# Attention pooling and a two-layer network on one core: another cut of the batch into chunks and groups, another order of the first loads, weighted sums moved to VectorE

## The chip, the core and the metric

One core of a Trainium2 chip runs the whole program. The metric is the device time of one execution in microseconds (us), the median of several. The engines are TensorE (PE in the profile, with its weight loads as PEld), VectorE (DVE), ScalarE (ACT), GpSimd (POOL) and SyncE (SP), which here only issues DMAs.

## What is computed

The input `x` has 4 batches of 12480 rows of 128 numbers; there are 32 inducing rows. Cut to what matters:

```python
def mab(q, kv):
    s = scale * (q @ kv.transpose(0, 2, 1))
    s = s - s.max(-1, keepdims=True)
    a = np.exp(s)
    a /= a.sum(-1, keepdims=True) + 1e-09
    return a @ kv
h = mab(I, x)            # 32 x 128 for each batch: a sum over all 12480 rows
y = mab(x, h)            # 12480 x 128 for each batch

t = y.reshape(49920, 128) @ w_in          # 128 x 2048
g = where(t >= 1, t, where(t <= -1, 0, (t + 1)**2 / 4))
out = g @ w_out                           # 2048 x 128
```

`h` of a batch needs the whole batch, so nothing of the second half can start on a batch before all its rows were read. `w_in` and `w_out` come as 64-bit floats and are made single precision on the chip.

## The kernel before, in words

**Chunks and groups.** A batch is cut into 25 chunks (`SIZES`, 15 of 512 rows and 10 of 480). Attention works on groups of up to four chunks (`GROUPS`), since 32 inducing rows fill a quarter of the 128 partitions: four chunks lie one below another and one instruction serves all. The seven groups have 4, 4, 4, 3, 4, 4 and 2 chunks. An instruction on a group costs by the width of a chunk, however many chunks there are.

**First half, `summarize`.** Chunks are loaded (`load`, L630), turned so that features lie on partitions (batch 0 by TensorE, L639, and a copy by ScalarE, L644; later batches by a strided load, L657, and VectorE, L660), scored against the inducing rows (`score`: L682 on TensorE, maximum L687 and bias L690 on VectorE, exponential L699 on ScalarE), and summed with these weights (`gather`: L725 turns the weights, L733 and L735 copy them, L741 multiplies, L748 copies the sum to `hs`). When all seven groups are in, a chain `c1` to `c12` merges them: the maximum over groups (L783, L786, L789), a bias for all (L796, L799), a factor for each group (L802), the total (L805, L806, L809), its inverse (L812, L813), a table of factors for each group (L816), seven matmuls that add the groups (L824), and a copy to `hT` (L828). `multiply` (L850) then forms `h @ w_in` once for the batch; its rounded and rest parts (L855, L858) are spread by 16 small DMAs (`spread`, L870) to the four tiles `hw` that the network's first matmuls take.

**Second half.** `attend` computes for each group the weights of its rows over `h`: L896 on TensorE, then L902, L908, L911 on VectorE, L916 on ScalarE, L919, L925, L933 on VectorE, L922, L928, L939 on GpSimd, L936 on ScalarE, and four DMAs for each chunk (L965) to the tile `aT`. The very first chunk has a shorter way of its own, `attend_first` (L987 to L1030). `chunk` then runs, for each of eight slices `k` of the hidden layer, two matmuls (L1083), their relu (L1091, ScalarE, one instruction for both where the two banks lie side by side, else two), the square (L1077, ScalarE), the bounds (L1096, VectorE, likewise one or two), a rounded part on one of three engines (L1116 GpSimd, L1120 ScalarE, L1122 VectorE), a rest (L1127, GpSimd), and the matmuls of the second layer (L1155); two of the eight slices skip the parts and multiply in full precision. L1167 and L1171 turn and store a chunk.

**What sets the order.** Nothing is ordered by data at run time: `Plan.order` plays the program through with a cost for each operation and gives each engine a fixed list. Among the operations that are ready, the one with the smallest due time goes first; due times come from the tables `DUE` (by kind of operation) and `SHIFT` (by number of a single operation). An engine, and the queue of DMAs on SP, then runs its list strictly in order. `SLOTS` says how many buffers a pool has; a load waits for its buffer. `keep_on` (L1184) adds matmuls of no use where the plan leaves TensorE idle, one each 250 ns from `WARM[0]` on.

**The weights.** `load_f32` reads 256 KB of 64-bit floats and makes 32-bit floats of them: L532 on ScalarE, L537, L540, L546, L552 and L557 on VectorE, L565 or L568 on GpSimd. `w_in` uses the buffers of `hw`, `aT` and `s2`, `w_out` those of the chunks (`w`, `hi`, `lo`), which in batch 0 also take the first loads of `x` (`FIRST`); `w_out` waits for chunk 16 (`after=got_all[0, 16]`). `mask` holds one of the six `hw` buffers until L1023.

## Time and profile before

| what | value |
|---|---|
| median of 3 runs | 1711.74 us (1711.71 to 1712.26) |
| profiled execution | span 1712.0 us from its first to its last instruction; its own time is one of those between 1711.71 and 1712.26 us, so that under 0.3 us lie around the span |
| busy | TensorE 99%, VectorE 95%, ScalarE 96%, GpSimd 95% of the span |
| first network matmul (L1083) | at 64.7 us |
| last stretch | from 1690 us on, TensorE busy 16.5 of 22 us |

The profile is read from its stages: a start in which the engines are loosely filled, until 64.7 us; a long stage in which all four are nearly full; an end of some 20 us. A busy share of TensorE counts matmuls that overlap in its pipeline, so that a full row is no proof that it has no room.

### The profile page before, as it was taken

Reading aid. Unit: us, or ns where it says so; the run is one execution under the profiler, and the core shown is the slowest. Engines: PE = TensorE matmul, PEld = TensorE weight load, DVE = VectorE, ACT = ScalarE, POOL = GpSimd, SP = SyncE. Lnnn points to the kernel's source line nnn. Section 1 sums busy time; section 2 is a strip of 40 time slices with the busy share of each in tenths; the row PEclk is TensorE's granted clock in tenths of the full one; section 3 lists DMA queues with packets and bytes.
Section 4 is the critical chain, followed back from the end, with each engine's and each line's share of the span. In section 5 each row is a group of like instructions: output and inputs, shape, how many; then the busy total and the mean of one; then the engine's idle time right before and its main releaser. Section 6 shows DMA issues by size and latency. Waiting matters only on the chain.

```text
span 1712.0 us, 25022 instructions
## 1 busy us (share of the span) xinstructions
PE 1690.1 (99%) x7716; PEld 1192.6 (70%) x7716; DVE 1633.7 (95%) x2119; ACT 1638.5 (96%) x2380; POOL 1621.4 (95%) x856
## 2 busy tenths in 40 slices
PE   7999999999999999999999999999999999999998
PEld 5756766677766667677776676667777766667776
DVE  5799999999899999999999999999999999999997
ACT  6699999999999999999999999999999999999997
POOL 2599999999999999999999999999999999999998
PEclk9899999999999999999999999999999999999999
DMA  9334433332343233333243333322212111111111
GB/s 275 87 54 81 79 61 65 54 75 50 66 79 74 48 72 66 59 59 70 50 96 54 74 66 69 60 56 55 41 31 58 30 33 36 28 36 36 33 32 18
DMA packets 427095, 105.66 MB, mean 62 GB/s; under 512 B 369842, under 2 KB 412434, under 8 KB 426962
## 3 DMA queue, kind: packets, MB, share of 16 engines
q1 hardware_dynamic: 425874, 103.82, 30.0%
q8 instruction: 61, 1.00, 0.3%
q14 instruction: 72, 0.59, 0.1%
q10 hardware_dynamic: 1088, 0.25, 0.1%
HBM read 48.94 MB, written 25.56 MB: 44 GB/s over the span
## 4 chain that ended last, share of the span: by engine, by line
PE 87%; DVE 6%; ACT 4%; issue 1%; DMA 1%; POOL 0%; SPq 0%; DVEq 0%; ACTq 0%; POOLq 0%
PE banks L1155 61%; PE banks L1083 19%; DVE w L1096 3%; ACT w L1091 2%; ACT w L1077 2%; DVE hi L1122 1%; PE banks L741 1%; PE banks L682 1%; PE banks L896 1%; PE banks L1184 1%; PE banks L725 1%; DMA w<-in_moe_w_out 1%; PE banks L639 1%; DVE oT L1167 1%; PE banks L824 0%
## 5 line engine op out<-in xcount | busy, mean ns | idle before, releaser
L1127 POOL TENSOR_TENSOR lo<-w,hi 128x1024 fp32r<-128x1024 f32 (+1 forms) x599 | 1394.1, 2360 | 20.4 <-PE banks L1155 5.2
L1096 DVE SCALAR_TENSOR_TENSOR w<-banks,w 128x512 f32<-128x512 f32 (+3 forms) x1159 | 953.2, 861 | 22.9 <-ACT w L1077 19.6
L1091 ACT ACTIVATE w<-banks 128x512 f32<-128x512 f32 (+3 forms) x1312 | 832.4, 704 | 22.7 <-PE banks L1083 20.1
L1077 ACT ACTIVATE w<-w 128x1024 f32<-128x1024 f32 (+1 forms) x800 | 826.9, 1068 | 3.1
L1083 PE MATMUL banks<-aT,hw 128*128 128x512 f32 (+1 forms) x1600 | 574.4, 429 | 3.0 <-DVE w L1096 2.1
L1155 PE MATMUL banks<-hi,w_lo 128*128 128x512 f32 (+1 forms) x1198 | 489.5, 409 | 2.9 <-DVE oT L1167 1.5
L1122 DVE TENSOR_REDUCE hi<-w 128x1024 fp32r<-128x1024 f32 (+1 forms) x406 | 474.0, 1176 | 10.8 <-PE banks L1155 1.5
L1155 PE MATMUL banks<-hi,w_hi 128*128 128x512 f32 (+1 forms) x1198 | 464.8, 388 | 0.0
L1155 PE MATMUL banks<-lo,w_hi 128*128 128x512 f32 (+1 forms) x1198 | 410.5, 428 | 0.1
L1083 PEld LDWEIGHTS banks<-aT,hw 128*128 128x128 f32 x1600 | 294.4, 188 | 151.5 <-DVE w L1096 58.8
L1155 PE MATMUL banks<-w,w_f 128*128 128x512 f32 (+1 forms) x804 | 392.1, 582 | 0.0
L1155 PEld LDWEIGHTS banks<-lo,w_hi 128*128 128x128 f32 x1198 | 222.8, 188 | 104.4 <-issue 52.5
L1155 PEld LDWEIGHTS banks<-hi,w_lo 128*128 128x128 f32 x1198 | 225.3, 188 | 83.6 <-issue 17.7
L1155 PEld LDWEIGHTS banks<-hi,w_hi 128*128 128x128 f32 x1198 | 225.5, 188 | 48.9 <-issue 9.9
L1155 PEld LDWEIGHTS banks<-w,w_f 128*128 128x128 f32 x804 | 151.0, 189 | 61.2 <-issue 37.8
L1116 POOL TENSOR_SCALAR hi<-w 128x1024 fp32r<-128x1024 f32 (+1 forms) x145 | 150.1, 1039 | 5.4 <-ACT s L916 0.8
L1167 DVE STREAM_TRANSPOSE oT<-banks 128x512 f32<-128x512 f32 (+1 forms) x100 | 69.3, 693 | 6.7 <-PE banks L1155 6.0
L660 DVE STREAM_TRANSPOSE xT<-xr 128x512 f32<-128x512 f32 (+1 forms) x75 | 50.7, 678 | 2.2 <-DMA xr<-in_x 2.2
L1120 ACT CAST hi<-w 128x1024 fp32r<-128x1024 f32 (+1 forms) x48 | 50.1, 1045 | 1.2 <-DVE w L1096 1.2
L939 POOL TENSOR_TENSOR a<-a,ahi 128x512 fp32r<-128x512 f32 (+3 forms) x28 | 35.7, 1276 | 2.1 <-ACT ahi L936 2.0
L568 POOL TENSOR_TENSOR w_in_sb<-aT,s 128x256 f32<-128x256 f32 x8 | 6.0, 752 | 31.9 <-DVE aT L557 31.9
L682 PE MATMUL banks<-xT,indT 128*32 128x512 f32 (+1 forms) x200 | 30.5, 612 | 0.0
(113 smaller groups left out, 574.6 us busy)
## 6 DMA issues: line engine op xcount, KB each, us to landing
out<-oT SPq DMA_DIRECT2D x240, 64.0 KB, 2.2
xn<-in_x SPq DMA_DIRECT2D x54, 256.0 KB, 4.1
xr<-in_x SPq DMA_DIRECT2D x180, 64.0 KB, 2.8
out<-oT SPq DMA_DIRECT2D x158, 60.0 KB, 2.2
aT<-ahi SPq DMA_DIRECT2D x118, 64.0 KB, 2.0
aT<-a SPq DMA_DIRECT2D x118, 64.0 KB, 2.0
xn<-in_x SPq DMA_DIRECT2D x30, 240.0 KB, 4.2
xr<-in_x SPq DMA_DIRECT2D x120, 60.0 KB, 2.6
```

The lines of the kernel that those rows point to most:

```text
L660: nc.vector.transpose(make(xT[b, c])[:, : CW[c]], xr.tile[:, : NB[c]].rearrange("c n i -> c (n i)"))
L682: nc.tensor.matmul(p[q * M : (q + 1) * M, :cw], indT, xT[b, c].tile[:, :cw], start=True, stop=True)
L1077: nc.scalar.activation(w.tile[:, :, :cw], w.tile[:, :, :cw], AF.Square, scale=0.5)
L1083: nc.tensor.matmul(make(h)[:, :cw], hw[b][ft // 4].tile[:, ft % 4 * P : (ft % 4 + 1) * P], aT[b, c].tile[:, :cw], start=True, stop=True,)
L1091: each(of, i, hs_, lambda h, to: nc.scalar.activation(to, h, AF.Relu, bias=1.0), cw, w)
L1096: lambda h, t: nc.vector.scalar_tensor_tensor(t, h, 1.0, t, op0=ALU.max, op1=ALU.min), cw, w,
L1116: nc.gpsimd.tensor_scalar(make(hi)[:, :, :cw], w.tile[:, :, :cw], 1.0, 0.0, op0=ALU.mult, op1=ALU.add)
L1120: nc.scalar.copy(make(hi)[:, :, :cw], w.tile[:, :, :cw])
L1122: nc.vector.tensor_reduce(make(hi)[:, :, :cw], w.tile[:, :, :cw].unsqueeze(3), axis=AX.X, op=ALU.max)
L1127: nc.gpsimd.tensor_sub(make(lo)[:, :, :cw], w.tile[:, :, :cw], hi.tile[:, :, :cw].bitcast(F32))
L1155: nc.tensor.matmul(acc.tile[:, :cw], wt[k][:, i, :], g.tile[:, i, :cw], start=first, stop=(acc.parts == 0),)
L1167: nc.vector.transpose(make(oT)[:, :nb].rearrange("c n i -> c (n i)"), acc.tile[:, :cw])
```

## The change

`SIZES` becomes one chunk of 448, sixteen of 512 and eight of 480 rows, and `GROUPS` the first chunk by itself and six full groups of four. In batch 0 the lone chunk keeps its own first way (now 448 wide), and the group attention starts with the next group. In batches 1 to 3 (`apart`) the lone chunk is laid on the four quadrants: `PARTS` and `QUARTER` cut it in four pieces of 128 columns, so that each instruction on it is 128 wide; its rows come by 14 small DMAs instead of one, its `aT` by 16 instead of 4.

The merging chain forms the sum over groups on VectorE (`gathered`, a product and six multiply-adds of 128 x 128, six of them before the last group is in) and then needs one matmul; the bias goes out by one matmul from a row of 128.

`w_out` is loaded to other buffers (`hw`, `aT`, `s2` for even slices, `xr`, `oT` for odd ones) and waits for no chunk; one step of the weights (`to_single`) may go to GpSimd. Loads of batch 1 may not be issued before 54 us of the plan. The plan takes 4.9 us for a first load where it took 3.2. In batch 0 the exponentials go to three buffers in turn. The 16 DMAs of `spread` may go to ScalarE's queue or SP's in batch 0. `keep_on` starts at 1.5 us. `DUE` is changed in most kinds, and `SHIFT` has 2436 entries where it had 880.

```diff
-SIZES = [512] * 15 + [480] * 10
-GROUPS = [[0, 1, 2, 3], [4, 5, 6, 7], [8, 9, 10, 11], [12, 13, 14], [15, 16, 17, 18], [19, 20, 21, 22], [23, 24]]
+SIZES = [448] + [512] * 16 + [480] * 8
+GROUPS = [[0]] + [[c, c + 1, c + 2, c + 3] for c in range(1, 25, 4)]
...
-WARM = (14000, 200)
+WARM = (1500, 250)
...
+    PARTS = [(0, 4), (4, 8), (8, 12), (12, 14)]
+    def apart(b, g):
+        return b > 0 and len(GROUPS[g]) == 1
...
-        made, f = load_f32(src, when, due, after=got_all[0, 16])
+        made, f, value = load_f32(src, when, due, pools=("xr", "oT", "oT") if k % 2 else ("hw", "aT", "s2"))
...
+        later = (54000 if b == 1 else 0, math.inf)
...
+                    def fetch_part(n, c=c):
+                        q, k = divmod(n, 4)
+                        to = (xn[c].tile or make(xn[c], [P, Q, C], F32))[k * M : (k + 1) * M, q, :]
+                        nc.sync.dma_start(to, x_cols(b, c)[:, n, :])
...
-            p1, e1[g] = Slot("h"), Slot("e1")
+            p1, e1[g] = Slot("h"), Slot("e1" if b else ["e1", "hx", "hy"][g % 3])
...
         def c4():
-            p = make(s_b)
-            for q in range(Q):
-                nc.tensor.matmul(p[q * M : (q + 1) * M, :1], mrow, one, start=True, stop=True)
+            nc.tensor.matmul(make(s_b)[:, :1], mrow, one, start=True, stop=True)
...
         def c10():
-            nc.vector.scalar_tensor_tensor(
-                ff, s_f.tile[:, :NG].unsqueeze(2).to_broadcast([P, NG, M]), rs,
-                fold[:, :1, :].to_broadcast([P, NG, M]), op0=ALU.mult, op1=ALU.mult,
-            )
-        def c11(groups):
-            p = s_h.tile or make(s_h)
+            nc.vector.tensor_scalar(share, fold[:, 0, :], rs, None, op0=ALU.mult)
+        def gathered(groups):
+            a = s_a.tile or make(s_a)
             for g in groups:
-                nc.tensor.matmul(p[:, :M], hs[:, g, :], ff[:, g, :], start=(g == 0), stop=(g == NG - 1))
+                to, by = whole if g == NG - 1 else a[:, :C], fr[:, g : g + 1]
+                if g == 0:
+                    nc.vector.tensor_scalar(to, hs[:, g, :], by, None, op0=ALU.mult)
+                else:
+                    nc.vector.scalar_tensor_tensor(to, hs[:, g, :], by, a[:, :C], op0=ALU.mult, op1=ALU.add)
+        def c11():
+            nc.tensor.matmul(make(s_h)[:, :M], whole, share, start=True, stop=True)
...
-            hw_made[b].append([
-                add("ACT" if b == k == r % 2 == 0 else "SP", 610, 2700, end + 3 + k,
+                ways = {e: (610, 2700, end + 3 + k) for e in (["SP"] if b else ["SP", "ACT"])}
...
+    QUARTER = [min(4 * q, CW[0] // M - 4) for q in range(Q)]
...
+            for q in range(rows // M):
+                c, i = (cs[0], QUARTER[q]) if split else (cs[q], 0)
                 nc.tensor.matmul(
-                    p[q * M : (q + 1) * M, :cw], hT[b], xT[b, c].tile[:, :cw], start=True, stop=True
+                    p[q * M : (q + 1) * M, :cw], hT[b], xT[b, c].tile[:, i * M : i * M + cw], start=True, stop=True
                 )
...
-        for g in range(NG):
+        for g in range(0 if b else 1, NG):
             attend(b, g, begins(b, GROUPS[g][0]))
```

Three places of the lists show what moves.

The first is the queue of loads on SP in the start, its last loads of batch 0. In a name, `in_x` is the input, `in_moe_w_in` and `in_moe_w_out` the weights; 96x640 is a chunk of batch 0 with 480 rows, 128x4x128 one of batch 1. Before:

```order
L630 DMA hi_367<-in_x 96x640
L527 DMA w_379<-in_moe_w_out 128x512
L527 DMA w_389<-in_moe_w_out 128x512
L527 DMA hw_402<-in_moe_w_in 128x512
L630 DMA w_413<-in_x 96x640
L630 DMA w_435<-in_x 96x640
L630 DMA lo_446<-in_x 96x640
L630 DMA w_460<-in_x 96x640
L630 DMA w_474<-in_x 96x640
L630 DMA lo_494<-in_x 96x640
L630 DMA xn_505<-in_x 128x4x128
L630 DMA hi_525<-in_x 96x640
```

And changed:

```order
L656 DMA hw_508<-in_moe_w_in 128x512
L778 DMA w_518<-in_x 96x640
L656 DMA hw_539<-in_moe_w_out 128x512
L656 DMA hw_550<-in_moe_w_in 128x512
L656 DMA hw_559<-in_moe_w_out 128x512
L656 DMA xr_575<-in_moe_w_out 128x512
L778 DMA w_581<-in_x 96x640
L778 DMA lo_595<-in_x 96x640
L656 DMA hw_620<-in_moe_w_out 128x512
L656 DMA xr_630<-in_moe_w_out 128x512
L656 DMA hw_669<-in_moe_w_out 128x512
L656 DMA xr_855<-in_moe_w_out 128x512
```

Eight chunks of batch 0 stood behind loads of `w_out`, and two of these (`hi_525` and one further down) behind a load of batch 1 as well; now three loads of `w_out` stand ahead of the last chunk, which is the 37th load, and none of batch 1.

The second is VectorE while the last groups of batch 0 are merged (L806 is the total, L816 the table of factors, L828 the copy to `hT`; between them lie steps of the weights). Before:

```order
L806 TENSOR_REDUCE tot_85<-fs_84 128x1
L546 SCALAR_TENSOR_TENSOR lo_818<-w_753,lo_818 128x256
L812 TENSOR_SCALAR rs_86<-banks 128x1
L813 RECIPROCAL rs_86<-rs_86 128x1
L816 SCALAR_TENSOR_TENSOR ff<-banks,rs_86,fold 128x224
L552 TENSOR_SCALAR hi_806<-lo_818 128x256
L557 SCALAR_TENSOR_TENSOR hi_806<-w_753,hi_806 128x256
L546 SCALAR_TENSOR_TENSOR s_162_798<-hw_730,s_162_798 128x256
L552 TENSOR_SCALAR aT_782<-s_162_798 128x256
L540 TENSOR_SCALAR lo_857<-hi_796 128x256
L828 COPY hT_860<-banks 128x32
```

And changed (L988 is the total, L1005 and L1007 are the weighted sums, L1014 is the copy; L681 to L692 are the steps that were L546 to L557):

```order
L988 TENSOR_REDUCE tot_85<-fs_84 128x1
L681 SCALAR_TENSOR_TENSOR oT_723<-xr_630,oT_723 128x256
L681 SCALAR_TENSOR_TENSOR s_146_757<-hw_559,s_146_757 128x256
L994 TENSOR_SCALAR rs_86<-banks 128x1
L995 RECIPROCAL rs_86<-rs_86 128x1
L998 TENSOR_SCALAR share<-fold,rs_86 128x32
L1005 TENSOR_SCALAR banks<-hs,fr_87 128x128
L1007 SCALAR_TENSOR_TENSOR banks<-hs,fr_87,banks 128x128 x5
L687 TENSOR_SCALAR aT_737<-s_146_757 128x256
L687 TENSOR_SCALAR oT_723<-oT_723 128x256
L692 SCALAR_TENSOR_TENSOR aT_737<-hw_559,aT_737 128x256
L1007 SCALAR_TENSOR_TENSOR whole<-hs,fr_87,banks 128x128
L692 SCALAR_TENSOR_TENSOR oT_723<-xr_630,oT_723 128x256
L1014 COPY hT_857<-banks 128x32
```

Six steps of the weights lie between the total and the copy in both; the seven sums over `hs` have come in among them.

The third is ScalarE between `multiply` and the first relu. Before (L855 rounds the product, L870 spreads it, L1005 is the exponential of the first chunk, L1026 the rounding of its `aT`):

```order
L1005 ACTIVATE s_179_884<-s_179_884 128x128
L855 CAST hx_891<-banks 128x512
L870 DMA hw_899<-hx_891 32x512 x2
L606 CAST w_hi_90<-hi_796 128x256
L606 CAST w_hi_93<-hi_621 128x256
L1026 CAST aT_932<-banks 128x512
```

And changed (the same are L1042, L1058, L1201 and L1225):

```order
L1042 CAST hx_878<-banks 128x512
L1058 DMA hw_887<-hx_878 32x512 x2
L1058 DMA hw_887<-hy_889 32x512 x2
L1058 DMA hw_898<-hy_889 32x512
L1058 DMA hw_898<-hx_878 32x512
L1058 DMA hw_891<-hx_878 32x512
L1201 ACTIVATE s_164_880<-s_164_880 128x128
L666 ACTIVATE oT_941<-xr_855 128x256
L741 CAST w_hi_95<-oT_729 128x256
L741 CAST w_hi_90<-aT_704 128x256
L1058 DMA hw_925<-hx_878 32x512
L741 CAST w_hi_97<-aT_734 128x256
L1225 CAST aT_976<-banks 128x448
```

Seven DMAs stand ahead of the first chunk's exponential on ScalarE where two stood behind it.

## Rows read from the trace of the kernel before

**Rows 1.** The page's first part: busy time of each engine, its share of the span, and its instructions.

```profile
PE 1690.1 (99%) x7716; PEld 1192.6 (70%) x7716; DVE 1633.7 (95%) x2119; ACT 1638.5 (96%) x2380; POOL 1621.4 (95%) x856
```

**Rows 2.** The windows view of the whole program in stretches: from and to (us), length, then for TensorE's matmuls and weight loads, VectorE, ScalarE and GpSimd the busy us and (x instructions), the granted clock (1.00 is 2.4 GHz, 0.50 is 1.2 GHz), the share of the DMA engines and what they moved.

```profile
20.00:45.00 25.00, 23.96 (x344) 16.44 (x345) 16.26 (x45) 19.24 (x50) 5.21 (x7) 1.00 0.93 267
...
48.00:59.00 11.00, 10.36 (x62) 7.83 (x62) 6.73 (x24) 1.81 (x7) 3.94 (x5) 0.53 0.01 1
59.00:65.00 6.00, 5.94 (x52) 4.82 (x49) 4.14 (x13) 2.23 (x5) 2.05 (x4) 1.00 0.31 82
65.00:100.00 35.00, 32.67 (x164) 22.45 (x163) 31.50 (x47) 32.05 (x47) 29.35 (x20) 1.00 0.48 90
100.00:1690.00 1590.00, 1586.36 (x6961) 1119.52 (x6960) 1550.52 (x1937) 1561.78 (x2238) 1563.29 (x806) 1.00 0.29 56
1690.00:1712.00 22.00, 16.54 (x62) 11.03 (x60) 11.93 (x14) 10.20 (x15) 13.97 (x7) 0.97 0.14 22
```

**Rows 3.** The waits view between 100 and 1690 us: who waited for whom, us in total, times, longest.

```profile
PEld banks L1083 <- DVE w L1096: 54.0, 180, 0.8
...
DVE w L1096 <- ACT w L1077: 18.8, 39, 1.3
...
ACT w L1091 <- PE banks L1083: 15.9, 32, 1.4
```

**Rows 4.** The chain that ended last, from 36 to 66 us, in order of time: start us, us, what.

```profile
37.41 1.02 PE banks L639 x10
...
38.98 0.99 PE banks L682 x8
...
40.05 0.67 DVE mg L687
...
41.02 0.76 ACT e L699 x2
...
42.15 4.73 DMA w<-in_moe_w_out
...
49.19 2.28 PE banks L741 x20
51.47 3.13 PE banks L824 x14
...
57.77 1.34 PE banks L850 x8
...
61.32 0.91 PE banks L1023 x8
...
63.62 1.07 PE banks L896 x8
64.69 1.12 PE banks L1083 x4
```

**Rows 5.** The timeline of SyncE's DMA queue in the first 76 us: start us, us that the issues took, and the loads.

```profile
7.38 6.48 SPq L630 DMA_DIRECT2D xn<-in_x  x9
...
16.92 1.00 SPq L630 DMA_DIRECT2D w<-in_x  x2
23.70 0.31 SPq L630 DMA_DIRECT2D lo<-in_x  x1
...
34.34 5.05 SPq L630 DMA_DIRECT2D xn<-in_x  x7
...
69.34 6.08 SPq L657 DMA_DIRECT2D xr<-in_x  x8
```

**Rows 6.** The windows view of two short stretches of the loads, columns as in group 2.

```profile
12.00:18.00 6.00, 5.91 (x29) 3.68 (x27) 4.00 (x12) 3.09 (x7) 1.48 (x2) 1.00 1.05 385
...
22.00:26.00 4.00, 3.95 (x60) 2.36 (x52) 2.17 (x7) 3.40 (x10) 0.00 (x0) 1.00 0.61 151
```

**Rows 7.** The timeline between 9.6 and 10 us, three pieces of VectorE and GpSimd: start us, us, engine, line, operation.

```profile
9.63 0.29 DVE L537 TENSOR_SCALAR aT<-aT 128x256 f32<-128x256 f32 x1
...
9.80 0.74 POOL L568 TENSOR_TENSOR w_in_sb<-aT,s 128x256 f32<-128x256 f32 x1 [8.51 <-DVE aT L557]
...
9.95 0.73 DVE L540 TENSOR_SCALAR s<-aT 128x256 uint32<-128x256 uint32 x1
```

**Rows 8.** The timeline of ScalarE between 57 and 61 us; ACTq is its issuing of DMAs.

```profile
57.53 0.31 ACT L1005 ACTIVATE s<-s 128x128 f32<-128x128 f32 x1 [4.17 <-DVE s L1002]
...
59.84 1.25 ACTq L870 DMA_DIRECT2D hw<-hx  x2
```

**Rows 9.** The groups of instructions between 100 and 1690 us: line, engine, operation, tiles, shapes, count | busy us, mean ns of one | idle time before them and its releasers.

```profile
L939 POOL TENSOR_TENSOR a<-a,ahi 128x512 fp32r<-128x512 f32 (+3 forms) x27 | 34.4, 1274 | 0.1
L928 POOL TENSOR_TENSOR s<-s,sm 128x512 f32<-128x512 f32 (+3 forms) x27 | 27.8, 1031 | 0.7 <-DVE sm L925 0.3 <-PE banks L1083 0.2
L896 PE MATMUL banks<-xT,hT 128*32 128x512 f32 (+1 forms) x184 | 26.9, 592 | 0.0
L741 PE MATMUL banks<-xn,eN 128*32 128x128 f32 (+1 forms) x600 | 22.6, 276 | 0.0
...
L911 DVE TENSOR_TENSOR s<-banks,mx 128x512 f32<-128x512 f32 (+3 forms) x26 | 17.1, 659 | 0.1
...
L733 DVE COPY eN<-banks 128x512 f32<-128x512 f32 (+2 forms) x12 | 7.9, 655 | 0.1
...
L733 ACT COPY eN<-banks 128x512 f32<-128x512 f32 (+3 forms) x9 | 4.9, 543 | 0.0
```

## What is predicted of the change

> **What bounds the kernel now.** Read first the busy shares: TensorE 99%, the three others 95 to 96% [rows 1]. Then the windows, which split the program in stages [rows 2]. Between 100 and 1690 us the engines are busy for 1586, 1551, 1562 and 1563 of 1590 us; ScalarE has 28 us of idle time, GpSimd 27, VectorE 39. No engine is alone the bound there: TensorE's weight loads wait 54 us for VectorE, VectorE 19 us for ScalarE, ScalarE 16 us for TensorE [rows 3]. A microsecond taken from one engine is worth part of a microsecond. The start is another matter. Until the first network matmul at 64.69 us [rows 4] it is a chain: the last chunk of batch 0 is turned at 37.4 us, scored in 0.99, its maximum found in 0.67, its exponential in 0.76; then the chain runs through a load of `w_out` of 4.73 us whose conversion stands ahead of the bias on VectorE; then L741 and the group sums L824, 2.28 and 3.13 us, at a granted clock of 0.53, which is mostly the 1.2 GHz level [rows 2, 4]. ScalarE and GpSimd were busy for only 1.8 and 3.9 us of those 11. What shortens this chain moves the whole rest forward.
>
> **The loads.** Before, nine loads were issued in 6.48 us, 0.72 us each, as fast as the transfers let them (385 GB/s between 12 and 18 us), but SP then stood still from 17.9 to 23.7 us, and the rate fell to 151 GB/s [rows 5, 6]: the loads of `x` share buffers with `w_out` and wait behind it, and seven loads of batch 1 went out at 34.3. In the new list the last chunk is the 37th load and shares no buffer with `w_out`. As before, 12 are issued by 7.4 us; 25 more at 0.72 end at 25.4; landing takes 4.7 [rows 4], so the last chunk is there at about 30. Bounds: 27 if all 9.3 MB came at 385 GB/s, 36 if SP stands still again for the 5.8 us of before, which could happen since three loads of `w_in` and two of `w_out` ahead of it wait for `hw` buffers that VectorE must free. I take 30: VectorE had such work before too, and was busy for 16.3 of 25 us with it [rows 2].
>
> **The chain to hT.** From 30.2: turning 1.0 for two chunks, copy 0.5, scores 1.0, maximum and bias 0.84 [rows 4]; conversions of `w_out` that stand ahead of the last exponential on ScalarE, taken at 1 (bounds 0 and the 4.73 us of a late load): 34.6. Then exponential 0.76, and for each of the two last groups 0.51 for turning (half of 1.02), 0.7 for the copies (one takes 0.54 [rows 9]), and L741 at full clock, half of 2.28: 2.35 each. The last of the seven sums, copies and one matmul in place of L824: five short steps, 1.2 together. Six of the sums (about 1.5 us, estimated from 0.66 us for four times the width [rows 9]) run on VectorE while the last group is being turned, so they cost nothing here; without that cover they would cost the 1.5. That makes 41.2. Two things are added. Waits at the hand-overs: 1 us, as before there were some. And VectorE against GpSimd: at 9.63 us a step of the weights took VectorE 0.29 us, the next, of the same size and begun while GpSimd worked from 9.80 on, took 0.73 and ended as GpSimd did [rows 7]. Six such conversions lie among the sums, with GpSimd now given more of them: bounds 0 and 6 x 0.44 = 2.6 us; I take 1, since only the two of the form that was held up in the row count fully. hT is there at about 43.2; before, L824 ended at 54.6.
>
> The Trainium skill (SBUF — State Buffer, "SBUF: two separate sides") says that VectorE and GpSimd share a pair of ports as an exclusive lock, held for a whole instruction, and that the loser waits; the row of 0.73 us agrees. By that rule taken strictly, the upper bound of 2.6 would hold and the time be 1.6 us later.
>
> **From hT to the first matmul.** The first chunk's scores 0.4, L850 1.0 (1.34 before, partly at the lower clock), rounding 0.6, then on ScalarE seven DMA issues at 1.25 / 2 = 0.62, 4.4 us, which now stand ahead of the exponential of 0.31 [rows 4, 8]. Behind it wait VectorE's five steps (1.6), L1023 (0.91), and rounding and rest (1.3). About 10.5 us, with hand-overs 11.5; before, 10.1. The six issues that left SP's queue save nothing that decides, since the exponential ends later than the spread. The first matmul starts at 43.2 + 11.5 = 54.7; I take 55 against 64.69, **9.7 us gained**, with bounds 4 and 13.
>
> **The ramp.** Chunk 0 has 448 rows instead of 512, so it covers an eighth less of its some 15 us while the next chunks' `aT` is made. SP issued eight strided loads of batch 1 in 6.08 us ahead of those fetches [rows 5]; the new list has ten of them and six small ones there. **2 us lost** (0 to 4).
>
> **The long stage.** The lone chunk takes the place of a group in batches 1 to 3, at a quarter of its width. TensorE: L896 takes 26.9 / 23 = 1.17 us a group (184 matmuls, 8 a group), the scores the same, L741 22.6 / 21 = 1.08 [rows 9]; three quarters of 1.17 + 1.17 + 1.08 + 0.5 for turning is 2.9, and L824 at full clock, 1.6 us, shrinks by 1.4. That is 4.3 us a batch, 13 in three, and 1.2 for the group that batch 0 no longer has: 14. VectorE: six instructions like L911, 0.66 us each, shrink to some 0.28: 2.3 a batch, 7; batch 0 3.3; seven copies to `eN` moved to ScalarE, 4.6; the sums cost 1.5 a batch, 4.5 [rows 9]: 10 less. GpSimd: L939 and L928, 2.3 us, by three quarters, and once in full: 7.5 less. ScalarE: three instructions like its L733 by three quarters, 1.2 a batch and 1.1 once, 4.7 less; seven copies of 0.54 more, 3.8; and by the lists 1146 single relus instead of 1024, 61 pairs split, at 46 ns (the start of one in the plan's cost line) 3: together 2 more. The mean over the four is -7.5. Since ScalarE gives nothing back, I take **6 us gained**; the ends are TensorE's 14 and ScalarE's loss of 2. The extra small DMAs, 25 a batch at 0.62 us, 16 us of SP's 410, hide behind chunks that were fetched earlier.
>
> **Sum.** 1712.0 - 9.7 + 2 - 6 = 1698.3 as a span; the median of the runs lies 0.3 below it: **1698 us**.
>
> **Rivals.**
> 1. The clock falls again in the merging chain. Before, it was granted 0.53 from 48 to 59 us after TensorE had stood with gaps [rows 2]; in the new chain TensorE works in pieces too, with few idle matmuls between them. Then L741, turning and L850 take twice their time: 4 us, 1702. Against it: idle matmuls from 1.5 us on, and shorter gaps. The Trainium skill (TensorE: Matmul & The Clock Gate, "Part 1: The HAM clock gate") says that the throttled clock is the default and activity releases it; the stretch of 0.53 agrees.
> 2. ScalarE sets the pace of the long stage: its load does not fall, so nothing comes of 6: 1704. For it, 96% busy and the split relus; against it, its waits for TensorE.
> 3. TensorE sets the pace: 14 instead of 6, 1690. For it, most of the chain that ended last; against it, the waits on VectorE.
> 4. The loads do not run through: SP stands still for `hw` buffers, x at 36 us, 1704.
> 5. Slower: relus and copies queue ahead of each other on ScalarE in the long stage, banks come free later, and TensorE stands. It decides where the long stage grows by the 7.7 us gained ahead of it and 3.4 more, 11 us; 2 are ScalarE's added load, so its idle time would have to grow from 28 to 37 us, by 0.1 us for each of 100 chunks. With a little more, 1716.
>
> **Chances.** Forecast 0.46, rivals in turn 0.15, 0.14, 0.12, 0.06, 0.07. The three runs differ by 0.6 us; 0.2%, 3.4 us, is about what can be told from no change. All but the last lie below 1708; giving 0.05 of the spread of these to within 0.2% and a part of the last: faster 0.87, same 0.06, slower 0.07. The range 1688 to 1708 takes in the first five and leaves out the last and the tails.
>
> **What would show it.** First matmul of the network at 52 to 58 us; last load of `x` landed by 31; granted clock 1.00 from 30 to 55; the merging chain free of any wait for `w_out`; in the long stage, groups of scores with a 128 wide one in each batch, and TensorE's matmul lines of attention 14 us shorter; about 28 us of ScalarE idle time or less. A first matmul after 60, or an idle time of ScalarE above 35 us, would make the prediction wrong.

## The result, and the profile after

The changed kernel takes 1722.1 us (median of four runs, 1721.0 to 1723.0), the kernel before 1712.0 beside it. By the ratio on record, 1.0069 with a 95% interval of 1.0053 to 1.0085, it is **slower by 0.69%**; these two medians alone make 0.59%. The forecast was 1698, 1688 to 1708. The profiled execution has a span of 1719.5 us and a time of its own of 1721.7.

The busy shares of the changed kernel, answering [rows 1]:

```profile
PE 1694.3 (99%) x7764; PEld 1193.5 (69%) x7764; DVE 1637.3 (95%) x2112; ACT 1645.8 (96%) x2446; POOL 1618.1 (94%) x862
```

Its windows, columns as in [rows 2]:

```profile
20.00:45.00 25.00, 24.47 (x352) 18.67 (x355) 18.82 (x55) 18.75 (x48) 6.81 (x12) 1.00 0.63 169
45.00:51.00 6.00, 5.58 (x69) 4.16 (x60) 5.48 (x16) 2.12 (x5) 3.09 (x4) 1.00 0.15 46
51.00:61.40 10.40, 9.71 (x85) 7.99 (x84) 9.12 (x23) 2.87 (x9) 5.84 (x8) 1.00 0.52 131
...
100.00:1690.00 1590.00, 1575.89 (x6868) 1104.09 (x6867) 1541.89 (x1914) 1556.24 (x2278) 1544.52 (x795) 1.00 0.29 56
```

The shares hardly differ; the windows do. The granted clock stays at 1.00 through the whole start, where it was 0.53 before. Between 100 and 1690 us every engine has *more* idle time: TensorE 14.1 us (3.6 before), VectorE 48 (39), ScalarE 34 (28), GpSimd 45 (27). What grew is not one engine's work.

Two numbers split the result. The first network matmul starts at 61.4 us, 3.2 earlier than the 64.6 before. From there to the end the kernel before takes 1647.4 us, the changed one 1658.1: **+10.7**. I call this time "the rest". To find where it is lost I took the progress of both kernels (columns of hidden layer whose relu is done) and asked how long the changed kernel takes for what the kernel before does in a given stretch:

| stretch of before, us | what it holds | changed kernel |
|---|---|---|
| 90 to 420 | batch 0 | -2.0 |
| 420 to 460 | **merging chain of batch 1** | **+2.1** |
| 460 to 840 | | +3.4 |
| 840 to 880 | **chain of batch 2** | **+1.3** |
| 880 to 1250 | | +1.6 |
| 1250 to 1295 | **chain of batch 3** | **+3.6** |
| 1295 to 1690 | | +2.2 |

In 125 us of batch ends 7.0 us are lost, in the 1475 us between them 5.2; 1.5 come back before 90 us and after 1690. The table has a grain, since the work on neighbouring chunks overlaps: read on the turning of each chunk's output (L1167 before, L1366 changed) the ends lose 5.9 us and the stretches between them 4.5. The third batch end shows how the ends lose it. Timeline of all engines in the changed kernel: start us, us, engine, line, operation, idle time before it and its releaser.

```profile
1270.44 2.25 POOL L1326 TENSOR_TENSOR lo<-w,hi 128x960 fp32r<-128x960 f32 x1 [0.18 <-ACT hi L1319]
1270.59 0.35 DVE L1005 TENSOR_SCALAR banks<-hs,fr 128x128 f32<-128x128 f32 x1
...
1270.98 1.92 DVE L1007 SCALAR_TENSOR_TENSOR banks<-hs,fr,banks 128x128 f32<-128x128 f32 x5
...
1272.66 0.99 POOL L1315 TENSOR_SCALAR hi<-w 128x960 fp32r<-128x960 f32 x1
1272.81 0.85 DVE L987 TENSOR_TENSOR fs<-fr,sg 128x7 f32<-128x7 f32 x1
...
1273.73 2.25 POOL L1326 TENSOR_TENSOR lo<-w,hi 128x960 fp32r<-128x960 f32 x1
1273.78 0.34 DVE L1007 SCALAR_TENSOR_TENSOR whole<-hs,fr,banks 128x128 f32<-128x128 f32 x1
1274.03 0.68 DVE L1366 STREAM_TRANSPOSE oT<-banks 128x480 f32<-128x480 f32 x1
...
1274.17 0.38 PE L991 MATMUL banks<-tot,fold 128*128 128x1 f32 x2 [1.42 <-DVE whole L1007]
...
1274.98 1.03 DVE L998 TENSOR_SCALAR share<-fold,rs 128x32 f32<-128x32 f32 x1
...
1275.94 1.14 DVE L1295 SCALAR_TENSOR_TENSOR w<-banks,w 128x960 f32<-128x960 f32 x1
```

From 1270.6 to 1275.9 VectorE does the chain and turns one chunk's output (L1366, 0.68 us): 5.35 us without one of the network's bounds (L1295), on which TensorE's weight loads wait most [rows 3]. Two of its steps are far longer than their size. `fs` has 128x7 numbers and takes 0.85 us; it ends (1273.66) when GpSimd's L1315 does (1273.65). `share` has 128x32 and takes 1.03; it ends (1276.01) with GpSimd's L1326 (1275.98). TensorE stands for 1.42 us on L991, which is ahead of the network's next matmuls in its list. Then the clock falls; the windows view of the next four us:

```profile
1276.00:1280.00 4.00, 4.00 (x24) 2.02 (x22) 3.16 (x7) 1.35 (x2) 1.51 (x2) 0.57 0.38 61
```

The granted clock is 0.57 there, mostly the 1.2 GHz level, after TensorE had been busy for 2.3 of the 4 us ahead of it. In the kernel before, VectorE's list at the same place interleaves (timeline of VectorE, kernel before):

```profile
1270.46 0.17 DVE L805 TENSOR_TENSOR fs<-banks,sg 128x7 f32<-128x7 f32 x1 [0.23 <-ACT banks L802]
1270.66 0.16 DVE L806 TENSOR_REDUCE tot<-fs 128x1 f32<-128x7 f32 x1
1270.74 1.87 DVE L1096 SCALAR_TENSOR_TENSOR w<-banks,w 128x480 f32<-128x480 f32 x3
1272.52 0.15 DVE L812 TENSOR_SCALAR rs<-banks 128x1 f32<-128x1 f32 x1
1272.70 0.16 DVE L813 RECIPROCAL rs<-rs 128x1 f32<-128x1 f32 x1
1272.90 0.45 DVE L816 SCALAR_TENSOR_TENSOR ff<-banks,rs,fold 128x224 f32<-128x224 f32 x1
```

`fs` takes 0.17 there, and the longest step 0.45: the factors lie in PSUM (`banks`), where the changed kernel has them in SBUF (`fr`).

### The profile page after: what moved, and what is told of

Read it like the earlier page. It is cut to its first block, busy times and chain, and to the rows that moved or that the text cites. A ratio compares the mean times of both kernels' runs of the same rounds, so it can differ in the third digit from the quotient of the medians.

```text
span 1719.5 us, 25317 instructions
## 1 busy us (share of the span) xinstructions
PE 1694.3 (99%) x7764; PEld 1193.5 (69%) x7764; DVE 1637.3 (95%) x2112; ACT 1645.8 (96%) x2446; POOL 1618.1 (94%) x862
## 4 chain that ended last, share of the span: by engine, by line
PE 75%; DVE 9%; ACT 8%; issue 4%; POOL 2%; SPq 0%; DMA 0%; DVEq 0%; ACTq 0%; POOLq 0%
PE banks L1354 53%; PE banks L1282 16%; DVE w L1295 4%; ACT w L1290 4%; ACT w L1276 3%; DVE hi L1321 2%; POOL lo L1326 2%; PE banks L918 1%; PE banks L1090 1%; PE banks L839 1%; DVE oT L1366 1%; PE banks L890 1%; PE banks L1383 1%; PE banks L788 1%; DVE banks L1007 0%
## 5 line engine op out<-in xcount | busy, mean ns | idle before, releaser
L1326 POOL TENSOR_TENSOR lo<-w,hi 128x1024 fp32r<-128x1024 f32 (+2 forms) x599 | 1392.8, 2357 | 26.3 <-DVE hi L1321 8.4
L1295 DVE SCALAR_TENSOR_TENSOR w<-banks,w 128x512 f32<-128x512 f32 (+5 forms) x1140 | 953.0, 875 | 31.0 <-ACT w L1276 24.7
L1290 ACT ACTIVATE w<-banks 128x512 f32<-128x512 f32 (+5 forms) x1373 | 839.3, 678 | 17.6 <-PE banks L1282 14.2
L1276 ACT ACTIVATE w<-w 128x1024 f32<-128x1024 f32 (+2 forms) x800 | 829.4, 1065 | 3.0
L1282 PE MATMUL banks<-aT,hw 128*128 128x512 f32 (+2 forms) x1600 | 584.1, 437 | 7.0 <-DVE w L1295 6.3
L1354 PE MATMUL banks<-hi,w_lo 128*128 128x512 f32 (+2 forms) x1198 | 496.2, 414 | 3.2 <-POOL hi L1315 1.2
L1321 DVE TENSOR_REDUCE hi<-w 128x1024 fp32r<-128x1024 f32 (+2 forms) x404 | 472.5, 1181 | 9.0 <-issue 0.4
L1354 PE MATMUL banks<-hi,w_hi 128*128 128x512 f32 (+2 forms) x1198 | 466.6, 390 | 0.0
L1354 PE MATMUL banks<-lo,w_hi 128*128 128x512 f32 (+2 forms) x1198 | 408.4, 418 | 4.3 <-DVE oT L1366 2.4
L1354 PE MATMUL banks<-w,w_f 128*128 128x512 f32 (+2 forms) x804 | 390.9, 582 | 0.0
L1315 POOL TENSOR_SCALAR hi<-w 128x1024 fp32r<-128x1024 f32 (+2 forms) x146 | 150.7, 1035 | 15.2 <-PE banks L1354 4.6
L1366 DVE STREAM_TRANSPOSE oT<-banks 128x512 f32<-128x512 f32 (+2 forms) x100 | 69.5, 695 | 8.2 <-PE banks L1354 7.1
```

The costliest lines, as they stand in the source:

```text
L1276: nc.scalar.activation(w.tile[:, :, :cw], w.tile[:, :, :cw], AF.Square, scale=0.5)
L1282: nc.tensor.matmul(make(h)[:, :cw], hw[b][ft // 4].tile[:, ft % 4 * P : (ft % 4 + 1) * P], aT[b, c].tile[:, :cw], start=True, stop=True,)
L1290: each(of, i, hs_, lambda h, to: nc.scalar.activation(to, h, AF.Relu, bias=1.0), cw, w)
L1295: lambda h, t: nc.vector.scalar_tensor_tensor(t, h, 1.0, t, op0=ALU.max, op1=ALU.min), cw, w,
L1315: nc.gpsimd.tensor_scalar(make(hi)[:, :, :cw], w.tile[:, :, :cw], 1.0, 0.0, op0=ALU.mult, op1=ALU.add)
L1321: nc.vector.tensor_reduce(make(hi)[:, :, :cw], w.tile[:, :, :cw].unsqueeze(3), axis=AX.X, op=ALU.max)
```

## The experiments

All ratios are to the kernel before, run beside it. "First" is the first network matmul and "rest" the time from it to the end, both of the profiled execution (profiles of before: the one of the front); "ends" are the three batch ends as in the table above, and "between" the four stretches between them together. A dash: the stretches were not taken there. The kernel before is run anew beside each series, and its median moves from 1709.3 to 1712.0 us, so that medians of different rows are not to be subtracted.

| run | ratio (95%) | median us | first | rest | ends | between |
|---|---|---|---|---|---|---|
| before | 1 | 1712.0 | 64.6 | 1647.4 | 0 | 0 |
| changed | 1.0069 (1.0053, 1.0085) | 1722.1 | 61.4 | 1658.1 | +2.1 +1.3 +3.6 | +5.2 |
| sums_on_pe | 1.0082 (1.0067, 1.0097) | 1724.5 | 64.0 | 1659.9 | +1.6 +1.2 +5.4 | +6.0 |
| no_hold | 1.0067 (1.0054, 1.0079) | 1721.7 | 62.0 | 1657.0 | +2.1 +1.3 +2.1 | +5.7 |
| share_psum | 1.0068 (1.0054, 1.0082) | 1720.7 | 61.5 | 1656.4 | +1.2 +1.5 +2.0 | +5.9 |
| share_split | 1.0068 (1.0055, 1.0080) | 1721.4 | 61.5 | 1657.8 | +0.9 +0.5 +4.7 | +6.0 |
| sums_psum | 1.0060 (1.0048, 1.0073) | 1722.0 | 63.4 | 1656.5 | +1.6 +1.6 +2.3 | +5.3 |
| bare_chain | 1.0040 (1.0027, 1.0052) | 1716.7 | 61.5 | 1652.7 | +0.3 -0.1 +0.8 | +6.1 |
| before_sums | 1.0131 (1.0117, 1.0145) | 1733.2 | 63.5 | 1666.3 | +3.6 +6.8 +6.8 | +1.9 |
| act_dose | 1.0056 (1.0043, 1.0069) | 1719.7 | 62.0 | 1656.2 | +2.1 +1.3 +2.1 | +5.0 |
| dve_dose | 1.0062 (1.0050, 1.0075) | 1720.5 | 61.6 | 1656.9 | +2.1 +1.2 +2.0 | +5.9 |
| pe_dose | 1.0043 (1.0030, 1.0057) | 1717.6 | 61.9 | 1653.5 | - | - |
| en_dve | 1.0084 (1.0069, 1.0099) | 1725.6 | 62.3 | 1660.9 | +1.6 +1.5 +2.1 | +9.9 |
| plain_before | 1.0250 (1.0235, 1.0264) | 1753.1 | 61.8 | 1690.2 | - | - |
| plain_after | 1.0302 (1.0287, 1.0317) | 1761.1 | 59.7 | 1702.4 | - | - |
| ind_first | 1.0079 (1.0063, 1.0094) | 1724.2 | 62.8 | 1659.3 | +2.1 +1.3 +3.6 | +6.5 |
| spread_sp | 1.0088 (1.0074, 1.0102) | 1725.6 | 66.0 | 1658.3 | +2.1 +1.3 +3.5 | +5.7 |
| x_first | 1.0072 (1.0059, 1.0085) | 1722.9 | 63.3 | 1658.2 | +2.1 +1.3 +3.6 | +5.5 |
| before_mend | 1.0001 (0.9992, 1.0011) | 1710.7 | 61.9 | 1646.8 | 0.0 +0.2 0.0 | -0.5 |
| before_idle | 1.0000 (0.9991, 1.0009) | 1710.0 | 63.7 | 1645.9 | 0.0 0.0 0.0 | -0.4 |

Cautions for reading it. The four runs of the changed kernel differ by 1.9 us, so 1 us in one row's "first" says little; what is worth reading is the rest. It too is that of one execution: the four kernels that differ in the start alone (changed, ind_first, spread_sp, x_first) have rests of 1658.1 to 1659.3, so that a few tenths say nothing. And the rest holds a coin: **at the third batch end the clock falls in some profiled executions and not in others**. It fell in the changed kernel, ind_first, spread_sp and x_first, whose third end costs 3.5 to 3.6, and stayed at 1.00 in no_hold, act_dose and dve_dose, where the same chain, with the same idle time of TensorE ahead of it, costs 2.0 to 2.1. The fall is worth 1.5 us. Without it the changed kernel's ends would cost 5.5 and its rest be 1656.6, and it is this that a variant with the clock up has to be compared with.

### The chain on VectorE

**sums_on_pe** puts the weighted sums back on TensorE, with seven factors from `fr` in SBUF:

```diff
-            nc.vector.tensor_scalar(share, fold[:, 0, :], rs, None, op0=ALU.mult)
+            nc.vector.scalar_tensor_tensor(ff, fr..., rs, fold..., op0=ALU.mult, op1=ALU.mult)
...
-                    nc.vector.scalar_tensor_tensor(to, hs[:, g, :], by, a[:, :C], ...)
+                nc.tensor.matmul(p[:, :M], hs[:, g, :], ff[:, g, :], ...)
```

> The weighted sums go back to TensorE (seven small matmuls at the place of the one), with every other instruction kept in its place in each queue. Theory A (VectorE's row of chain steps at the three later batch ends holds up bounds, and with them ScalarE and TensorE): the changed kernel falls behind by 6.5 us more than the kernel before in the chunks around 450, 865 and 1275 us; half or more of it comes back, 3 to 7 us, so 1715 to 1719, although TensorE gets 11 us of matmuls more. Theory B (ScalarE, busy for 8 us more, sets the pace of the long stage): ScalarE's work is the same, no change within 1 us, 1721 to 1723. Theory C (TensorE sets it): slower by 3 to 11 us, 1725 to 1733.

None of the three: the rest grew by 1.8, with the clock down in both. `ff` took 0.45, 0.79, 2.17 and 2.31 us in the four batches, `fs` 2.12 in the last. The undo had replaced one held step by a longer one, since the factors stayed in SBUF.

**no_hold** writes `fs` and `share` as another instruction:

```diff
-            nc.vector.tensor_mul(fs, fr, sg)
+            nc.vector.scalar_tensor_tensor(fs, fr, 1.0, sg, op0=ALU.mult, op1=ALU.mult)
...
+            nc.vector.scalar_tensor_tensor(share, fold[:, 0, :], rs, fold[:, 0, :], op0=ALU.mult, op1=ALU.mult)
```

> Only the form of two small steps of VectorE changes: L987 (0.41 and 0.85 us in the last two batch ends, 0.14 in the first) and L998 (1.24, 2.16 and 1.03 us; 0.24 in batch 0) become scalar_tensor_tensor, the form of L1007, whose times did not vary (0.35 to 0.36 us). If they were held up by GpSimd, whose instruction ends within 0.05 us of theirs, they take 0.15 to 0.3 us now: 4.6 us of VectorE over three batch ends. Theory A: 2 to 4 us of it come back, 1718 to 1720. Theory B: within 1 us, 1721 to 1723. If GpSimd was not the cause, the two steps keep their times and nothing changes.

`share` took 1.25, 2.16 and 1.05 us, as before the edit, `fs` up to 0.85; the 1.1 us by which the rest is shorter are the clock, which did not fall. The kind of instruction isn't what holds these steps; the place of their operands was tried next.

**share_psum** gives `share` an operand in PSUM:

```diff
-            nc.vector.reciprocal(rs, rs)
+            nc.vector.reciprocal(s_t.tile[:, 1:2], rs)
+            nc.vector.tensor_mul(share, s_t.tile[:, 1:2].to_broadcast([P, M]), fold[:, 0, :])
```

> The small step L998 took 1.24, 2.16 and 1.03 us at the three later batch ends and each time ended within 0.05 us of an instruction of GpSimd; as a scalar_tensor_tensor with both operands in SBUF it did the same (1.25, 2.16, 1.05). Here it reads the reciprocal from PSUM and stands right behind L995. Theory P (VectorE is held only where all its operands lie in SBUF): about 0.2 us each, 3.7 us of VectorE gone at places where TensorE and ScalarE wait for VectorE, 2 to 4 us back: ratio to before 1.0045 to 1.006. Theory Q (any small step there is held): its time stays near 1 to 2 us, ratio 1.006 to 1.0075.

The same place in its timeline (VectorE and GpSimd):

```profile
1272.51 0.99 POOL L1316 TENSOR_SCALAR hi<-w 128x960 fp32r<-128x960 f32 x1
1272.67 0.85 DVE L987 TENSOR_TENSOR fs<-fr,sg 128x7 f32<-128x7 f32 x1
...
1273.59 2.25 POOL L1327 TENSOR_TENSOR lo<-w,hi 128x960 fp32r<-128x960 f32 x1
...
1274.85 0.19 DVE L996 TENSOR_TENSOR share<-banks,fold 128x32 f32<-128x32 f32 x1
```

GpSimd's instruction runs from 1273.59 to 1275.84 as it did, and `share` passes beside it in 0.19 us; it took 0.19 in all four batches. `fs`, untouched, is still held. **The hold is shown.** Its price is small: the clock was up here, so the ends' 4.7 are to be held against 5.5, and the removal on this step was worth 0.8 us, little more than the table's grain.

**share_split** adds to that: five of the sums are not issued in a row but one behind each of VectorE's next instructions.

```diff
+            spaced[p] = [lambda g=g: gathered([g]) for g in range(1, NG - 1)]
...
             op.emit()
+            if op in spaced:
+                rest, stop = spaced[op], flush[op]
+            elif rest and op.engine == "DVE":
+                rest.pop(0)()
```

> As share_psum, and in batches 1 to 3 the six sums of one piece (2.3 us of VectorE in a row, 0.39 each) are issued one by one, one behind each of VectorE's next instructions. Theory A (VectorE's row of chain steps holds up the bounds behind it): 1 to 3 us more than share_psum come back, ratio 1.003 to 1.005. Rival (VectorE's total is what counts there, not the row): as share_psum, within 1 us.

At two ends it took what was hoped for, +0.9 and +0.5; at the third `fs` came to stand beside another of GpSimd's instructions, was held for 1.86 us, and the clock fell: +4.7. Less the 1.5 of the clock that is 4.6 at the three ends, no better than share_psum: what spacing gained at two, the hold took at one.

**sums_psum** has the sums on TensorE with factors that are made through PSUM:

```diff
+            nc.vector.tensor_scalar(rate, fr, rs, None, op0=ALU.mult)
+            nc.vector.tensor_mul(ff, rate..., fold...)          # rate in PSUM
```

> The changed kernel with the weighted sums on TensorE again, as in sums_on_pe, but the weights ff made right behind L995 from rates that stand in PSUM, as the kernel before had its exponentials in PSUM; nothing is left out. In sums_on_pe this step took 0.79, 2.17 and 2.31 us at the three later batch ends, held by GpSimd, and the undone part brought nothing back. Theory A: ff takes 0.45 us each time, the three batch ends lose 1 to 3 us in all instead of 7, from the first network matmul to the end 1653 to 1655.5, ratio 1.004 to 1.0055. Rival: fourteen matmul instructions in a row on TensorE cost what VectorE gains, 1657 to 1660, ratio 1.0065 to 1.008.

```profile
1271.98 2.25 POOL L1326 TENSOR_TENSOR lo<-w,hi 128x960 fp32r<-128x960 f32 x1 [0.19 <-ACT hi L1319]
1272.13 2.13 DVE L986 TENSOR_TENSOR fs<-fr,sg 128x7 f32<-128x7 f32 x1
...
1275.27 2.26 POOL L1326 TENSOR_TENSOR lo<-w,hi 128x960 fp32r<-128x960 f32 x1
...
1275.72 0.39 DVE L997 TENSOR_TENSOR ff<-banks,fold 128x224 f32<-128x224 f32 x1
```

In this timeline `ff`, 32 times as large as `fs`, passes GpSimd in 0.39 us, and `fs` waits 2.13 for it. The ends cost 5.5, what they cost in the changed kernel with the clock up, and the rest is the same (1656.5 against 1656.6). With 14 matmuls in a row (1.6 us) on TensorE and a held `fs`, taking the sums off VectorE brings nothing back.

**bare_chain** leaves the chain's work out instead: in batches 1 to 3 only two of the seven sums; in all batches no product for `fs`, and `share` from PSUM.

```diff
-            nc.vector.tensor_mul(fs, fr, sg)
-            nc.vector.tensor_reduce(tot, fs, axis=AX.X, op=ALU.add)
+            nc.vector.tensor_reduce(tot, fr, axis=AX.X, op=ALU.add)
...
-            for g in groups:
+            for g in groups if b == 0 else [0] if 0 in groups else [NG - 1]:
```

> The changed kernel with share_psum's step, and with less of VectorE's chain in the three later batch ends: of the seven sums only the first and the last are made, and tot is summed without its product (so the output is not the reference's). VectorE has 2.0 us less in a row at each of the three batch ends, and no small step there can be held. From the first network matmul to the end the changed kernel took 1658.1 us, share_psum 1656.4, the kernel before 1647.4. Theory A (VectorE's chain steps at the batch ends are what costs there, 7 us of the loss lies in 125 us around them): 1650 to 1653. Theory L (the order of the new list costs it, the steps hardly): 1655 to 1657.

The three ends now cost +0.3, -0.1 and +0.8, and the rest is 1652.7, 3.9 below 1656.6. Read on the turned outputs, the ends lose 4.3 in no_hold, with the clock up, and nothing here. The loss at the batch ends is the merging chain's: its sums, its long `share` and its `fs` together, of which only `share` was also taken alone. The loss between the ends, +6.1, is untouched by it and has another cause.

**before_sums** makes the opposite test: the kernel before, with the sums, `fr` and `share` of the changed one and nothing else; they are issued where the plan had the seven matmuls.

```diff
-            nc.scalar.activation(make(s_f)[:, :NG], mg, AF.Exp, bias=nm, scale=SCALE)
+            nc.scalar.activation(fr, mg, AF.Exp, bias=nm, scale=SCALE)
...
-                nc.tensor.matmul(p[:, :M], hs[:, g, :], ff[:, g, :], start=(g == 0), stop=(g == NG - 1))
+                    nc.vector.scalar_tensor_tensor(to, hs[:, g, :], by, a[:, :C], op0=ALU.mult, op1=ALU.add)
```

> The kernel before with one part of the change alone: the weighted sums on VectorE, with fr, share and the sums' result in SBUF as in the change, at the places in VectorE's queue that the matmuls' issue had; every other instruction in its place. From the first network matmul to the end the kernel before took 1647.4 us. Theory A (this part costs the long stage 5 to 7 us): 1652 to 1655. Theory L: 1647 to 1649.5. In batch 0 the chain may end up to 1 us earlier or later.

It is slower by 1.3%, and 17.2 us of the loss lie at the three ends; the four stretches between together lose 1.9. The timelines of VectorE and of GpSimd at its second end, and the waits there (engine and tile waited for: us in total, times, longest):

```profile
861.29 1.98 DVE L818 TENSOR_SCALAR share<-fold,rs 128x32 f32<-128x32 f32 x1
863.19 0.34 DVE L825 TENSOR_SCALAR banks<-hs,fr 128x128 f32<-128x128 f32 x1
863.57 1.92 DVE L827 SCALAR_TENSOR_TENSOR banks<-hs,fr,banks 128x128 f32<-128x128 f32 x5
865.40 2.28 DVE L1101 SCALAR_TENSOR_TENSOR w<-banks,w 128x480 f32<-128x480 f32 x3
```

```profile
860.99 4.41 POOL L1132 TENSOR_TENSOR lo<-w,hi 128x960 fp32r<-128x960 f32 x2 [0.48 <-ACT w L1096]
```

```profile
PE banks L829 <- DVE whole L827: 5.7, 1, 5.7
```

`share` is held until about when the first of GpSimd's two ends, the sums follow, and TensorE, whose list has the one matmul on `whole` ahead of the network's, stands still for 5.7 us. Behind the stands at the three ends the granted clock fell as well (0.62 from 452 to 456 us, 0.50 from 868 to 872 and from 1292 to 1296), so a part of the 17.2 is the clock's; how large a part was not measured. The same chain costs 17.2 us in lists that know nothing of it, with the clock down at all three ends, and in those of the changed kernel 7.0 with it down at one and 5.5 with it up; the kernel before pays nothing of the kind.

### One engine too many?

Three doses take a little from every instruction of a kind, so that the lists stay the same.

```diff
# act_dose
-  nc.scalar.activation(w.tile[:, :, :cw], w.tile[:, :, :cw], AF.Square, scale=0.5)
+  nc.scalar.activation(w.tile[:, :, : cw - 6], w.tile[:, :, : cw - 6], AF.Square, scale=0.5)
# dve_dose: the bounds, cw - 6 wide
# pe_dose: the matmuls on w_lo, 24 columns fewer
+  n = cw - 24 if wt is w_lo and not first else cw
```

> ScalarE's 800 squares leave the last 6 of each half's columns unsquared (1.00 us for 960 elements, so 12 elements are 0.0105 us each): 8.4 us less of ScalarE, spread evenly, and every instruction in its place. Those columns of the output are not the reference's. Theory B (ScalarE's 8 us more of busy time set the slower pace of the long stage): 6 to 8.4 us come back, 1714 to 1716, a ratio to before of about 1.002 to 1.003. Theory L (the order of the changed kernel lets all four engines wait for one another, none is the bound): 1 to 4 us, ratio 1.0045 to 1.006.

> VectorE's 1140 bounds leave out the last 6 columns of each half (0.64 us for 480: 1600 halves by 0.0063 us are 10 us of VectorE less), all else in place; those columns of the output are not the reference's. Theory A2 (VectorE's waits and busy time at the batch ends set it): 5 to 10 us come back, ratio about 1.001 to 1.004. Theory B (ScalarE sets the pace): within 1.5 us, ratio 1.006 to 1.0075. Theory L: 1 to 4 us, ratio 1.0045 to 1.006.

> The changed kernel with the 1198 matmuls of hi by w_lo (but the first of a chunk) 24 columns shorter, 0.010 us each by the 0.22 us between two of 512: 12 us of TensorE less, all else in place (output not the reference's). Rival 3 of the prediction (TensorE sets the pace): 8 to 12 us back, ratio to before 1.000 to 1.002. Theory L (waits go round all engines): 1 to 4 us back, ratio 1.0045 to 1.006; from the first network matmul to the end 1654 to 1657.

The clock was up at the third end in act_dose and dve_dose, so 1656.6 is their base: 8.4 us less of ScalarE shorten the rest by 0.4, 10 less of VectorE lengthen it by 0.3. In pe_dose the clock fell, to 0.91 over 15 us at the third end; 12 less of TensorE shorten the rest by 4.6 against the 1658.1 with a fallen clock. By the ratios, which take in all runs, act_dose lies 0.0013 below the changed kernel, dve_dose 0.0007 and pe_dose 0.0026: 2.2, 1.2 and 4.4 us, the first two within the intervals. So neither ScalarE nor VectorE sets the pace: a microsecond of ScalarE is worth 0.05 to 0.25, one of VectorE 0 to 0.1, one of TensorE about 0.4. GpSimd had no dose. Added work of ScalarE does not explain the loss: the 7.2 us that it is busy longer on the work that the kernel before does from 90 to 1690 us would, at 0.05 to 0.25 each, be 0.4 to 1.8.

**en_dve** tests the copies to `eN` that the change moved to ScalarE; on top of sums_psum, those of batches 1 to 3 go back to VectorE.

```diff
-  copy = nc.scalar.copy if v.engine == "ACT" else nc.vector.tensor_copy
+  copy = nc.scalar.copy if v.engine == "ACT" and b == 0 else nc.vector.tensor_copy
```

> As sums_psum, and in batches 1 to 3 the copies to eN that the change gave to ScalarE are issued by VectorE at the same places (0.68 us each there, 0.54 on ScalarE). Theory B (ScalarE's added work is the rest of the loss, between the batch ends): 1 to 3 us less than sums_psum. Theory L (the rest is in the order's waits; act_dose returned a quarter of what it took away): within 1 us of sums_psum or up to 2 us more.

The rest is 4.4 us longer than that of sums_psum. In these lists, moving them was right.

**plain_before** and **plain_after** empty `SHIFT` in each kernel; plain_after also has the due times of before for all kinds that both have.

```diff
-SHIFT = { "ACT": { 257: -557144, ... } ... }
+SHIFT = {}
```

> The kernel before, its work and due times as they are, without its table of single shifts of due times (SHIFT empty): its order comes from the due times alone. Theory L (the order, not the work, decides the few tenths of a per cent): slower than before by 10 us or more, 1722 to 1760. Theory S (the order matters little): within 4 us, 1708 to 1716.

> The changed kernel's chunks, groups, sums, loads and start, with the due times of the kernel before for the long stage and no table of single shifts, so that its long stage is ordered by the very rules of the run plain_before. Theory L (what the change does to the work is a gain or nothing, its own list of due times and shifts loses it): faster than plain_before by 4 to 15 us. Theory S (the work as the change cuts it, ScalarE's above all, is what costs in the long stage): slower than plain_before by 3 us or more.

plain_before loses 25 to 28 us in the ramp, which hides the comparison of totals. From the turning of chunk 4's output to the end of the program it takes 1565.6 us, plain_after 1588.7 from the same row on. Under these due times the changed work is 23 us worse, and it falls behind chiefly at batch changes (12 us between chunks 48 and 52). The tuned lists of the changed kernel gain 30 us on plain ones (1588.7 to 1558.6), those of before 20 (to 1545.6), so the tables of the change did not gain less than those of before. That the changed work is harder to order is not shown by this: the due times that both plain runs share were made for the kernel before.

### The start

**ind_first** issues the load of the inducing rows first, **x_first** the last three loads of `x` ahead of the loads of weights between them, **spread_sp** all sixteen DMAs of `spread` on SP.

```diff
# ind_first
+    done.sort(key=lambda op: op is not ind_in)
# x_first
+    late = [op for op in loads if op in x_loads][-3:]
+    ahead = loads[loads.index(late[0]) - 1]      # the three go behind this one
# spread_sp
-                queue = nc.scalar if by[0].engine == "ACT" else nc.sync
+                queue = nc.sync
```

> The load of the inducing points is issued first again instead of fifth; all else stays in place. In the changed kernel indT is there at 7.5 us and ScalarE's first copy begins at 9.04; before, 3.0 and about 5.8. Theory S1 (the late indT delays ScalarE's conversions, these the release of the buffers on which SP stands, and so the whole start): first copy at about 6, last x turned 2 to 3 us earlier than 35.1, first network matmul at 58 to 59.5 instead of 61.4, total 1719 to 1720. Theory S2 (the loads or the chain behind them decide): first copy earlier, but first network matmul at 61 or later, total 1721.5 to 1723.

`indT` was made at 7.08 instead of 7.47 us, the first copy at 8.65 instead of 9.04, where S1 needed about 6; so S1 was hardly put to the test, and nothing came of the 0.4 us.

> In the changed kernel the last three loads of x are issued at 24.0, 26.8 and 27.5 us, behind loads of the weights for which SP waits until VectorE has freed a buffer (23.6, 25.0, 26.0). Here these three are issued ahead of the first such load; all else keeps its place. Theory S5 (this stand of SP is what made the chain late: the last x copied at 36.4, hT at 47.6 to 50 in the five profiles so far): the three are issued by 22, the last x copied at 31 to 34, hT at 43 to 46, and all of the gain is kept to the end: ratio to before 1.0035 to 1.005. Theory S6 (the chain waits for VectorE's conversions or for ScalarE's copies anyway): hT at 47 or later, ratio 1.006 to 1.0075.

The loads of `x` were all issued by 23.9 us and landed by 31.5 (35.0 in the changed kernel), but the last copy to `xT` came at 38.1 (36.4 in the changed kernel). Timeline of ScalarE:

```profile
32.03 0.43 ACT L666 ACTIVATE aT<-hw 128x256 f32<-128x256 f32 x1 [2.38 <-DMA hw<-in_moe_w_in]
32.36 1.00 ACT L793 COPY xT<-banks 128x480 f32<-128x480 f32 x2
```

A conversion of `w_in`, whose load had gone behind, stands ahead of those copies in ScalarE's list: 2.38 us of waiting. An earlier landing with the weights' loads where they were was not tried.

> All sixteen spreads of batch 0 are issued by SP instead of eight by ScalarE; every other instruction keeps its place. ScalarE's exponential of the first attention waits 4.8 us behind these issues in the changed kernel (54.61 instead of 49.8). Theory S3 (this wait is on the path to the first network matmul): exponential at about 50, first network matmul at 57 to 58.5 instead of 61.4, total 1717 to 1719.5. Theory S4 (the conversions on VectorE and GpSimd up to 70 us, or SP's queue with eight issues more ahead of the loads of batch 1, decide behind it): first matmul earlier, but chunk 0 done at 91.5 or later (92.4 by rows in the changed kernel is 90.2 for its first chunk), total 1721 to 1724.

With SP alone the exponential of the first chunk came 2.2 us after `hT` instead of 7.0, but the sixteen issues on SP ended at 63.8 and the load of `w_out` behind them landed at 65.8, so that the first matmul came 16.0 us after `hT` instead of 13.8.

**before_mend** and **before_idle** take the kernel before and only mend its start: the first issues two conversions of `w_out` on ScalarE and steps of them on VectorE behind the chain's steps and adds three idle matmuls, the second adds eleven idle matmuls in the merging chain.

```diff
# before_mend
+    move([437, 427], 391)
+    move([438, 428, 429, 430], 403)
+    move([439], 406)
# before_idle
+    for ahead, more in ((395, 4), (397, 2), (401, 5)):
+        at_ = done.index(by_index[ahead])
+        done[at_:at_] = [by_index[117]] * more
```

> The kernel before, all work as it is: around the merging chain of batch 0 two conversions of w_out on ScalarE and four steps of them on VectorE are issued behind the chain's steps instead of ahead, and three idle matmuls more stand before L809. The conversions waited for a load (4.73 us at 42.15) and the chain behind them; and the clock fell to its lower level at 48 us. Expected: nm at 46 instead of 47.6, hT at 50 to 52 instead of 54.8, first network matmul at 60 to 62 instead of 64.6, and the same gain at the end, 3 to 4.5 us: ratio 0.9975 to 0.9985. Rival: the conversions, now later, hold up the first network chunk: no gain, ratio 0.9995 to 1.001.

> The kernel before with eleven idle matmuls more, in TensorE's gaps from 43.5 to 48.6 us. Of 36 runs of the kernel before, 22 have a mean granted clock of 0.999 or 1.000 and take 1707.9 to 1710.5 us, 14 have 0.996 to 0.998 and take 1710.0 to 1714.8; the profile of before is of the second kind. Theory K (in these 14 the clock fell in the merging chain, and this is all their difference): no run below 0.999, all between 1707.5 and 1710.5, ratio to before about 0.999. Rival (the extra matmuls stand in the chain's way): clock up, time not, ratio 1.000 or more.

Both are equal to the kernel before, though the first matmul of before_mend's profile came at 61.9. What they changed is the clock: over the five series of runs the kernel before had a mean granted clock of 0.999 or 1.000 in 39 of 61 runs (1707.3 to 1711.7 us, median 1708.9) and of 0.996 to 0.998 in 22 (1710.0 to 1714.8, median 1712.2); in before_mend (12 runs, median 1710.7) and before_idle (11 runs, median 1710.0) it was never below 0.999. So the fallen clock between 48 and 59 us [rows 2] is a matter of about a third of the runs, it costs them 3 us, and the profiled one was of that third. The medians of the two edits lie 1.8 and 1.1 us above the 1708.9 of the other two thirds, so that they cost about what the clock gives back. No version tried beats the kernel before.

## Why the prediction was wrong

**The loads: wrong by 5 us.** The last load of `x` was to land at 30 us; in the trace it landed at 35.0. SyncE's queue in the changed kernel (start us, us of the issues, loads):

```profile
11.20 1.00 SPq L778 DMA_DIRECT2D xn<-in_x  x2
15.55 0.33 SPq L778 DMA_DIRECT2D w<-in_x  x1
...
20.10 0.42 SPq L778 DMA_DIRECT2D w<-in_x  x1
23.58 0.35 SPq L656 DMA_DIRECT2D hw<-in_moe_w_in  x1
...
27.52 0.33 SPq L778 DMA_DIRECT2D lo<-in_x  x1
```

It was issued at 27.5, not 25.4: SP stood still from 12.2 to 15.5 for a buffer that TensorE freed, and from 20.5 to 23.6 for VectorE. And it took 7.4 us to land, for which the forecast took the 4.7 of a load of weights. The DMA view (tiles, queue, count, KB each, median us from issue to landing) has it in this line:

```profile
lo<-in_x SPq DMA_DIRECT2D x2, 240.0 KB, 7.0
```

So rival 4, with `x` at 36 us, came true within 1 us, less than half of the delay by its stand of SP and the rest by the landing.

**The chain to hT: 43.2 predicted, 47.6 measured, 54.6 before.** The chain of waits of the changed kernel (start us, us, what):

```profile
35.09 1.02 PE banks L788 x10
...
43.56 0.27 DVE banks L1005
43.85 0.37 DVE banks L1007
...
45.49 0.35 DVE banks L1007
...
52.02 0.61 ACTq L1058
...
54.62 0.31 ACT s L1201
```

The six sums that "cost nothing here", because the last group would be turned beside them, stand behind the whole last group instead, in a row on the path: 2.4 us (L1005 and five L1007). That did not make the chain longer than forecast: from the turning of the last chunks (L788, at 35.09, right after the last landing) to `hT` it took 12.5 us, where 13.0 were predicted from 30.2 on. The sums' time was paid by luck, out of the three allowances of 1 us each. The 4.4 missed are thus the late start of the chain; x_first, where the loads landed at 31.5 and the turning still began only at 37.0, behind ScalarE's wait for `w_in`, shows that an earlier landing alone need not bring the chain forward.

**From hT to the first matmul: 11.5 predicted, 13.8 measured.** The mechanism was right up to the exponential: it (54.62) waits for ScalarE's DMA issues, until 7.0 us after `hT`. Behind it the sum left out two terms. The rest of the first chunk's `aT` (L1229) starts at 58.9, 0.8 us after its rounded part was there, since conversions of weights stand ahead of it on VectorE. Then TensorE's list has the scores of two groups ahead of the first network matmul (timeline of TensorE), 1.85 us, where before it had one group in 1.07 [rows 4]:

```profile
59.57 1.92 PE L1090 MATMUL banks<-xT,hT 128*32 128x512 f32 x16 [0.69 <-DVE aT L1229]
61.42 1.28 PE L1282 MATMUL banks<-aT,hw 128*128 128x448 f32 x5
```

That the six issues that left SP "save nothing that decides" was wrong: spread_sp, which gives SP back all eight of ScalarE's, lost 2.2 us by it.

**The start together: 9.7 predicted, 3.2 between the two profiles, about 1 between the medians.** The runs of the kernel before have 1.8 us around their span, not the under 0.3 that was taken, those of the changed one 2.2. The profiled execution of before, with 1712.0 of span, is then one of some 1713.8, above the four runs beside it, and the reading that "the median lies 0.3 below" the span was wrong. With the rest of 1647.4, the median of 1712.0 has its first matmul at 62.8, and that of the changed kernel (1722.1, rest 1658.1) at about 61.8. The forecast took one execution's granted clock of 0.53 [rows 2] for the kernel's own; it is so in a third of the runs.

**The ramp: a loss of 2 predicted.** There was none; the changed kernel is 4.4 us ahead after the first chunk and 5.7 after chunk 20.

**The long stage: 6 gained predicted, 10.7 lost; this is the step that failed.** (The 10.7 is the rest, ramp and end with it.) The two parts of it failed in different ways.

*The savings were there, and little came of them.* The lines that answer to [rows 9], changed kernel, 100 to 1690 us:

```profile
L1090 PE MATMUL banks<-xT,hT 128*32 128x512 f32 (+2 forms) x192 | 23.4, 560 | 0.0
L918 PE MATMUL banks<-xn,eN 128*32 128x128 f32 (+1 forms) x576 | 19.4, 276 | 0.0
...
L1105 DVE TENSOR_TENSOR s<-banks,mx 128x512 f32<-128x512 f32 (+2 forms) x24 | 14.8, 616 | 0.1
```

The attention is 3.5 and 3.2 us lighter in the first two lines and 2.3 in the third, about as costed. But the same groups over the whole program, before and after, show where TensorE's saved time went:

```profile
L1083 PE MATMUL banks<-aT,hw 128*128 128x512 f32 (+1 forms) x1600 | 574.4, 429 | 3.0 <-DVE w L1096 2.1 <-DVE banks L902 0.5 <-DMA hw<-hy 0.2
...
L824 PE MATMUL banks<-ff,hs 128*128 128x32 f32 x56 | 8.6, 302 | 0.0
```

```profile
L1282 PE MATMUL banks<-aT,hw 128*128 128x512 f32 (+2 forms) x1600 | 584.1, 437 | 7.0 <-DVE w L1295 6.3 <-DVE s L1105 0.2
...
L1010 PE MATMUL banks<-share,whole 128*128 128x32 f32 x8 | 1.4, 254 | 0.4 <-DVE whole L1007 0.4
```

The sums are 7.2 us lighter, and 1600 matmuls on the same number of columns are busy 9.7 us longer and idle 4 us longer ahead; what holds them longer was not taken apart. From the first network matmul on, the times of its instructions added up, TensorE has 1.5 us less where 14 were predicted, VectorE 3 where 10 were, GpSimd 9 (predicted 7.5), ScalarE 5 more (2). Of ScalarE's the relus grew by 6.1, for which 3 were taken. My 6 us were a mean over four engines, as if each gave back a fraction of its saving; the doses put that fraction at about 0.4 for TensorE and near nothing for VectorE and ScalarE.

*The cost was in a term that I sized as busy time.* "The sums cost 1.5 a batch" on VectorE. Even as busy time they take 2.6 (0.35, 1.92 and 0.34 us at the third end). Above all they are links of a chain for which TensorE's list holds a place, and they run in a row, with bounds of the network behind them: the three ends lose 5.5 us with the clock up and 7.0 with it down at one, of which bare_chain returns all but 1.0. Part of that is the hold. I had it from [rows 7] and priced it for conversions in the start only; `fs` and `share`, with all operands moved to SBUF by the very change, I did not price at all. In the last batches' chains it took 0.85 us for 128x7 and up to 2.16 for 128x32 numbers.

**The rivals.** The fifth, slower at 1716 for want of banks, had the sign and nearly the size, not the mechanism: it turned on ScalarE's idle time, and that grew to 34 us, short of its 37; en_dve shows that the copies on ScalarE are a gain. The point "idle above 35" did not trip, the point "first matmul after 60" did, at 61.4, and the last `x` landed at 35.0 instead of by 31. Rival 1 (clock falls in the merging chain of the start) did not happen in this profile; at the third batch end it did. Rival 2 is refuted by act_dose. Rival 3 is half true, 0.4 a microsecond. Rival 4 came true in the loads, not in the total. None of the five had the batch ends.

**What stays open.** The 5.2 us between the batch ends are in every variant of the changed kernel (5.0 to 6.5, en_dve apart) and nearly absent in before_sums (1.9), so they belong neither to the sums nor to the start. They go with idle time on all engines; between 460 and 840 us the waits of weight loads for GpSimd's `lo` are 7.0 us (2.1 before) and those of the relus for TensorE 4.7 (1.1). That fits lists that mesh less well, as plain_after suggests, but this is not shown: the lone chunk, its small DMAs and the split relus (1373 for 1312) were not taken out one at a time, and GpSimd, whose idle time grew most (45 us for 27), had no dose. What makes the clock fall in one execution and not in the next was not found either.

## What to carry to other kernels

When work moves into a chain that ends a stage, price the chain's whole stretch on its engine's list and the instruction of another engine that waits for its end, not the busy time of the steps; here a term of 4.5 us of busy time, 7.8 as measured, stood against ends that lost 5.5 to 7.0 us in all. Where four engines are full, give a microsecond saved on one of them no value until a dose has shown one. Take the landing of a load from a row of the same load under the same traffic: 4.7 taken from another row were 7.4. Before a forecast takes a disturbed stretch of a profile as something to be gained, compare the profiled execution with the other runs: a third of this kernel's runs had the fallen clock, and 3 us of the promise were theirs.

## What the runs showed of the hardware

A short VectorE instruction whose operands all lie in SBUF did not end before a GpSimd instruction that had begun ahead of it: `fs` (128x7) took 0.14 us at its shortest and 0.85, 1.86 and 2.13 behind one, `share` (128x32) 0.24 and up to 2.16, `ff` (128x224) 0.45 and up to 2.31. With one operand in PSUM, `share` took 0.19 us and `ff` 0.39 in every batch, and the sums (L1007, `hs` from SBUF and the running total in PSUM) 0.34 to 0.39 beside the same GpSimd instructions. The Trainium skill (SBUF — State Buffer, "SBUF: two separate sides") says that a VectorE instruction with two SBUF inputs (against a GpSimd instruction that reads SBUF), or in a two-port mode, is locked out for the whole of a GpSimd instruction that began first, and (the same page, "Who interferes with whom") that one with at most one SBUF input outside those modes does not contend. The trace agrees for `fs` and `ff`, and for the steps with an operand in PSUM; whether `share` with one tensor in SBUF runs in a two-port mode no run shows.

The granted clock of one program differs from run to run: for the kernel before its mean was lower in a third of 61 runs, at 3 us each, in the profiled one of these by the 0.53 of the start; and at the third batch end it fell in four of the seven kernels that have the same chain there (changed, ind_first, spread_sp and x_first, not no_hold, act_dose and dve_dose), at 1.5 us.
